# Block 0's tokens kept in pair order through the attention output, with split stores

## The chip, the cores and the metric

The kernel runs on one NeuronCore of a Trainium2 chip. The metric is the device time of one execution in microseconds; what is compared is the median over several runs. The engines are TensorE (PE in the profile, its weight loads PEld), VectorE (DVE), ScalarE (ACT), GpSimd (POOL) and SyncE (SP); each works through its own queue in order, and they wait for one another by semaphores.

## The reference, cut to what matters

Attention with a decay per head runs in blocks over 768 tokens (batch 4, 8 heads of 64), and its output goes through a gated feed-forward layer.

```python
Dmask = np.where(rel >= 0, lam[:, None, None] ** rel[None, :, :], 0.0)      # rel = i - j
for b in range(nb):
    intra = np.einsum('bhic,bhjc->bhij', qb, kb) * Dmask[None]
    intra = np.einsum('bhij,bhjd->bhid', intra, vb)
    inter = np.einsum('bhid,bhde->bhie', qb * lam_pow[None], kv_state)
    out[:, :, sl] = intra + inter
    kv_state = lam_block[None, :, None, None] * kv_state + np.einsum('bhsd,bhse->bhde', kb_dec, vb)
x = np.ascontiguousarray(attn_out.transpose(0, 2, 1, 3)).reshape(B * S, H * D)
gate = 1.0 / (1.0 + np.exp(-(x @ w_gate)))
val = x @ w_val
return gate * val @ w_out                                                     # 3072 x 512
```

The weights are 512 x 1536 (gate and value) and 1536 x 512 (out). The decay is a power of the token distance, so the kernel may use blocks of another size than the reference's 64.

## The kernel before, in words

The tokens are cut into six blocks of 128 (`NSTEP`), each for all four batch rows, so one block is 512 tokens wide in the feed-forward part (`TCH`). The order of all work is written out by hand: the calls at the end of the kernel are emitted in this order, and every engine works through its own part of it.

For blocks 1 to 5 there are pieces: `piece_t` (transposes or scaled queries), `piece_s` (scores), `piece_m` (scores times the decay mask), `piece_a` (value products into `XT`), `c` (state), `piece_gv` (gate and value products, sigmoid, product: one of 12 feature tiles `ft`), and `piece_po` (out projection of one batch row `tt`, an ACT copy into `ob`, and one store on SP's queue).

Block 0 is on its own, since everything waits for it at the start. Its rows are loaded by `load0` with two neighbouring tokens in one partition: partition s of batch row b holds tokens 2s and 2s+1 (`R = 2`, index r), and two batch rows share the 128 partitions (half i of pair bp). `turn0` transposes 64x64 pieces on TensorE (L267), so the columns of a transposed tile are in "pair order": all r = 0 tokens, then all r = 1 tokens. `scale0` (L277, DVE) scales queries by `lam0`, which is in pair order, and `piece_tk0` copies keys (L282, ACT). `piece_s0` makes the scores of one pair of batch rows: 32 products of 64x64 by 64x128 (L295) into four PSUM banks `S0[bp, e, u]`. Its right side is the scaled query tile read with a stride, so that the score columns come out in natural token order. `piece_m0` multiplies by `mask0` (L309 on DVE, or L306 on ACT and L307 on POOL) into `M0[bp]`; `mask0` is made by `make_mask0` from `tri0` (L157). `piece_a0` makes the value products of a pair, again 32 products (L323), in groups of `w` of the four 128-feature groups `m = 2x + u`, and copies them to `XT[0]` (L327 ACT, L328 ACT or DVE).

`idle(n)` emits n products of a zero tile into a scratch bank `wm` (L234, 128x128 by 128x512), which nothing reads. `preload_act_table_set` (L563) loads ACT's table for the sigmoid. PSUM tiles come from two pools, `ps_at` (5 banks, `AT`) and `ps_ff` (3 banks, `FF`). The start, from the second score block to the first gate product:

```python
    piece_s0(1)
    piece_m0(1, 0, 0, True)
    piece_m0(1, 0, 1)
    piece_m0(1, 1, 0)
    piece_m0(1, 1, 1)
    load_w(WV, wv_r, 1, GW)
    piece_a0(0, NMT, [AT, FF])
    idle(3)
    piece_a0(1, 2, [AT] * 4)
    nc.scalar.preload_act_table_set("sigmoid_and_others")
    make_mask(1)
    idle(2)
```

After it come loads on POOL's queue and `gv(0, 0, ..., 6)`, the first gate and value products (L463, L469). Block 0's four output tiles are stored much later, after block 1's gate products.

Of the kernel before, what the change touches and what calls it, by code (L numbers as in the profile page):

```python
# [8 lines left out]
FP32 = mybir.dt.float32  # L9
BF16 = mybir.dt.bfloat16  # L10
AF = mybir.ActivationFunctionType
ALU = mybir.AluOpType
# [4 lines left out]
def kernel(  # L17
# [11 lines left out]
    nc = tc.nc  # L29

    B, H, S, D = q.shape
    C = 128
# [5 lines left out]
    NMT = DM // 128  # L38
# [17 lines left out]
        engines={ET.PE, ET.Pool, ET.DVE, ET.Activation, ET.SP}))  # L56
# [31 lines left out]
    def load_w(t, src, i, w):  # L88
        fs = slice(i * w, (i + 1) * w)
        nc.gpsimd.dma_start(out=t[:, :, fs], in_=src[:, :, fs])  # L90
# [9 lines left out]
    R = 2  # L100
    SR = C // R
    Q0, K0, V0 = (qkv.tile([128, NB2, H, R, D], BF16, tag=c + "b", name=c + "b") for c in "qkv")
# [20 lines left out]
    ip1 = const.tile([128, C], FP32, tag="ip1")  # L123
    nc.vector.memset(ip1[:, 0:1], 1.0)  # L124
    w = 1
# [14 lines left out]
    for r in range(R):  # L140
        nc.vector.tensor_scalar(out=tok[:, 2 + r:3 + r], in0=tok[:, 1:2], scalar1=float(R),
                                scalar2=float(r + 1 - R), op0=ALU.mult, op1=ALU.add)
        nc.vector.tensor_scalar(out=tok[:, 4 + r:5 + r], in0=tok[:, 2 + r:3 + r], scalar1=-1.0,
                                scalar2=None, op0=ALU.mult)
    p1, tj, ntj = tok[:, 0:1], tok[:, 2:4], tok[:, 4:6]
# [5 lines left out]
    for i, src in enumerate((p1, tj[:, 0:1], tj[:, 1:2])):  # L151
        nc.vector.tensor_scalar(out=rem[:, i:i + 1], in0=src, scalar1=-1.0, scalar2=float(C),
                                op0=ALU.mult, op1=ALU.add)
    tri0 = const.tile([128, R, C], FP32, tag="tri0")
    ipr = ip1.rearrange("p (s r) -> p r s", r=R)
    for r in range(R):
        nc.vector.tensor_scalar(out=tri0[:, r], in0=ip1, scalar1=tj[:, r:r + 1], scalar2=None,  # L157
                                op0=ALU.is_ge)

    lnr = const.tile([128, 2, 2, 2], FP32, tag="lnr")  # L160
    for e in range(2):
# [7 lines left out]
    for u in range(2):  # L169
        us = slice(u * 64, (u + 1) * 64)  # L170
# [21 lines left out]
    def make_mask0(e, u):  # L192
        a = 4 * e + 2 * u
        nc.vector.tensor_tensor(
            out=mask0[:, e, u], in0=tri0.unsqueeze(1).to_broadcast([128, 2, R, C]),
            in1=pk0[:, a:a + 2].unsqueeze(3).to_broadcast([128, 2, R, C]), op=ALU.mult)
# [5 lines left out]
    def make_lamq(gs):  # L202
        for g in gs:
            nc.scalar.activation(lamq[:, g], ip1, AF.Exp, scale=lnp[:, g:g + 1])
# [4 lines left out]
    def make_mask(u):  # L209
        nc.vector.tensor_tensor(  # L210
            out=mask[:, u].rearrange("p (e x) c -> p e x c", e=2),
            in0=tri.unsqueeze(1).unsqueeze(1).to_broadcast([128, 2, 2, C]),
            in1=pk.rearrange("p (e u x) -> p u e x", e=2, u=2)[:, u].unsqueeze(3).to_broadcast([128, 2, 2, C]),
            op=ALU.mult)

    def half(e):
        return slice(e * 64, (e + 1) * 64)
# [12 lines left out]
    def idle(n, fresh=False):  # L230
        if fresh:
            wm[0] = ps_ff.tile([128, TCH], FP32, name="wm", tag="ff")
        for i in range(n):
            nc.tensor.matmul(wm[0], lhsT=zero[:, :128], rhs=zero, start=True, stop=True,  # L234
                             skip_group_check=True)

    QS, KS, MT, XT, KD = {}, {}, {}, {}, {}
# [33 lines left out]
    def piece_tq0(b, pool=ps_at, tag="ps"):  # L271
        tp = turn0(Q0, b, pool, tag)
        QS[0, b] = QS0[:, b]
        TQ[b] = tp
# [4 lines left out]
    def piece_tk0(b, pool=ps_at, tag="ps"):  # L279
        tp = turn0(K0, b, pool, tag)  # L280
        KS[0, b] = KS0[:, b]
        nc.scalar.copy(KS[0, b], tp)  # L282

    S0, M0, TQ = {}, {}, {}

    def piece_s0(bp):
        for e in range(2):
            for u in range(2):
                S0[bp, e, u] = ps_at.tile([128, 2, R, C], FP32, name="sp", tag="ps")
        for e in range(2):  # L290
            for x in range(2):
                for r in range(R):
                    for i in range(2):
                        for u in range(2):
                            nc.tensor.matmul(S0[bp, e, u][half(i), x, r, :],  # L295
                                             lhsT=KS[0, 2 * bp + i][half(u), 2 * e + x, r * SR:(r + 1) * SR],
                                             rhs=QS[0, 2 * bp + i][half(u), 2 * e + x, :].rearrange("p (r s) -> p s r", r=R),
                                             start=(x == 0 and r == 0), stop=(x == 1 and r == R - 1),
                                             skip_group_check=True)
        M0[bp] = trsb.tile([128, 2, 2, 2, R, C], BF16, tag="QR", name="MT0", bufs=2)  # L300

    def piece_m0(bp, e, u, pool=False):
        sp = S0[bp, e, u]
        if pool:
            sc = const.tile([128, 2, R, C], FP32, tag="sc", bufs=2)
            nc.scalar.copy(sc, sp)  # L306
            nc.gpsimd.tensor_tensor(out=M0[bp][:, e, u], in0=sc, in1=mask0[:, e, u], op=ALU.mult)  # L307
        else:
            nc.vector.tensor_tensor(out=M0[bp][:, e, u], in0=sp, in1=mask0[:, e, u], op=ALU.mult)  # L309

    def piece_a0(bp, w, banks):
        if 0 not in XT:
            XT[0] = xtp.tile([128, NMT, B, C], BF16, tag="XT", name="XT")
        for m0 in range(0, NMT, w):
            op = []
            for i in range(2):
                pool, tag = banks.pop(0)
                op.append(pool.tile([128, w, C], FP32, name="op", tag=tag))
            for m in range(m0, m0 + w):
                for r in range(R):  # L320
                    for e in range(2):
                        for i in range(2):
                            nc.tensor.matmul(op[i][half(e), m - m0, :], lhsT=V0[half(i), bp, 2 * m + e, r, :],  # L323
                                             rhs=M0[bp][half(i), e, m % 2, m // 2, r, :],
                                             start=(m == m0 and r == 0), stop=(m == m0 + w - 1 and r == R - 1),
                                             skip_group_check=True)
            nc.scalar.copy(XT[0][:, m0:m0 + w, 2 * bp, :], op[0])  # L327
            (nc.vector.tensor_copy if bp else nc.scalar.copy)(XT[0][:, m0:m0 + w, 2 * bp + 1, :], op[1])  # L328

    def piece_t(n, bp):  # L330
        if n > 1:
# [173 lines left out]
    def piece_po(n, tt):  # L505
        po = ps_ff.tile([128, DM], FP32, name="po", tag="ff")
        for ft in range(NFT):
            nc.tensor.matmul(po, lhsT=HT[n, ft][:, tt * 128:(tt + 1) * 128],  # L508
                             rhs=WO[:, ft, :], start=(ft == 0), stop=(ft == NFT - 1))
        ob = osb.tile([128, DM], FP32, tag="ob", name="ob")  # L510
        nc.scalar.copy(ob, po)  # L511
        dst = out[tt * S + n * C:tt * S + (n + 1) * C, :]
        nc.sync.dma_start(out=dst, in_=ob)


    GW = DFF // 6
# [2 lines left out]
    FF = (ps_ff, "ff")  # L519
    AT = (ps_at, "ps")  # L520
# [9 lines left out]
    make_mask0(1, 0)  # L530
    make_tri()
    make_mask(0)
    idle(4)
    piece_tq0(1)
    scale0(1)
    make_mask0(1, 1)
    idle(2)
    piece_tk0(1)
    make_lamq((2, 3))
    idle(1)  # L540
    piece_tq0(2, *FF)
    scale0(2)
    piece_tq0(3, *FF)
    scale0(3)
    piece_s0(0)
    piece_m0(0, 0, 0)
    piece_m0(0, 0, 1)
# [4 lines left out]
    piece_tk0(3, *FF)  # L552
    idle(2, True)
    piece_s0(1)
    piece_m0(1, 0, 0, True)
    piece_m0(1, 0, 1)
    piece_m0(1, 1, 0)
    piece_m0(1, 1, 1)
    load_w(WV, wv_r, 1, GW)
    piece_a0(0, NMT, [AT, FF])  # L560
    idle(3)
    piece_a0(1, 2, [AT] * 4)
    nc.scalar.preload_act_table_set("sigmoid_and_others")  # L563
    make_mask(1)
    idle(2)

# [61 lines left out]
    gvh(1, 1, 0, 1, 2, 3, 4, 5, 6)  # L628
    gv(1, 7, 8, 9, 10, 11)
    piece_po(0, 0)  # L630
    piece_po(0, 1)
    piece_po(0, 2)
    t(2, 0)
    t(2, 1)
# [72 lines left out]
```

## Time and profile before

| what | value |
|---|---|
| median of 6 runs | 231.24 us (230.3 to 231.82) |
| profiled execution, its own time | 231.99 us |
| its span, first to last instruction | 230.2 us, mean granted TensorE clock 0.992 |
| TensorE busy | 220.6 us, 96% of the span |
| DVE, ACT, POOL busy | 102.5, 82.6, 81.0 us |
| score products of block 0 (L295) | 64, 2.7 us busy |
| value products of block 0 (L323) | 64, 2.3 us busy |
| idle products (L234) | 20 recorded, 7.8 us busy, mean 507 ns |
| stores of whole output tiles (L513) | 23 of 256 KB, 2.0 us to landing (median) |

"Busy" is the time in which an engine had an instruction in work; products overlap, so the sum of their own durations is larger. The granted clock is the share of full TensorE clock that was granted in a stretch. The chain of waits goes back from the last instruction, at each step to what released it. "Issue" in it is time in which the engine waited for nothing that the profile shows. A few matmul records may be missing.

### The profile page before, as it was taken

What the parts mean: (1) busy time and instruction counts of PE and PEld (TensorE: products, weight loads), DVE (VectorE), ACT (ScalarE), POOL (GpSimd) and SP (SyncE); (2) the same over time, 40 slices, a digit from 0 to 9 for tenths busy, and PEclk for the clock granted to TensorE, in tenths of its full rate; (3) what the DMA queues carried; (4) which work ended last, traced back from release to release, by engine and by line L of the source; (5) the groups of instructions that cost most, each with busy time, mean ns of one, the idle gap of its engine ahead of it and who ended that gap; (6) DMA issues with size and microseconds to landing.
All of it is one profiled execution on the core that took longest, in us unless ns stands there. A gap on an engine that the chain in (4) does not pass through costs nothing.

```text
span 230.2 us, 4618 instructions
## 1 busy us (share of the span) xinstructions
PE 220.6 (96%) x1921; PEld 113.6 (49%) x1947; DVE 102.5 (45%) x189; ACT 82.6 (36%) x157; POOL 81.0 (35%) x77
## 2 busy tenths in 40 slices
PE   7869999999999999999999999999999999999993
PEld 2635454688544446444446444445444445444442
DVE  7857366484441342334842334842334840334200
ACT  5655324544332224333224433224433225333220
POOL 8979997854950003970003970000000000000000
PEclk9979999999999999999999999999999999999999
DMA  7999999999999912799912899912730012100022
GB/s 67 155 186 156 171 193 159 199 178 157 132 158 154 235 65 77 162 154 147 40 61 80 169 136 146 54 57 82 166 63 3 0 53 86 46 0 0 3 91 93
DMA packets 96517, 24.95 MB, mean 108 GB/s; under 512 B 85616, under 2 KB 93552, under 8 KB 96496
## 3 DMA queue, kind: packets, MB, share of 16 engines
q0 software_dynamic: 76112, 14.16, 89.3%
q1 hardware_dynamic: 20384, 10.49, 19.8%
q8 instruction: 15, 0.25, 0.5%
q14 instruction: 6, 0.05, 0.1%
HBM read 28.32 MB, written 6.29 MB: 150 GB/s over the span
## 4 chain that ended last, share of the span: by engine, by line
PE 92%; DMA 2%; POOL 2%; issue 2%; ACT 1%; DVE 0%; POOLq 0%
PE po L508 26%; PE gp L463 25%; PE vp L469 24%; PE gp L480 3%; PE vp L486 2%; PE sp L356 2%; PE op L384 2%; DMA qb<-in_q_dram 2%; PE op L374 1%; PE po L497 1%; POOL qb L105 1%; PE sp L295 1%; PE cp L450 1%; PE op L323 1%; PE wm L234 1%
## 5 line engine op out<-in xcount | busy, mean ns | idle before, releaser
L472 DVE TENSOR_TENSOR ht<-sg,vp 128x512 bf16<-128x512 bf16 x65 | 44.7, 687 | 76.0 <-PE vp L469 71.8
L463 PE MATMUL gp<-XT,WG 128*128 128x512 bf16 x252 | 66.2, 379 | 0.7 <-issue 0.2
L469 PE MATMUL vp<-XT,WV 128*128 128x512 bf16 x255 | 65.8, 379 | 0.1
L466 ACT ACTIVATE sg<-gp 128x512 bf16<-128x512 f32 x65 | 38.8, 597 | 69.6 <-PE gp L463 69.5
L508 PE MATMUL po<-WO,ht 128*128 128x512 bf16 x266 | 61.3, 379 | 0.5
L508 PEld LDWEIGHTS <-ht 128*128 128x128 bf16 x276 | 26.3, 98 | 31.2
L469 PEld LDWEIGHTS <-WV 128*128 128x128 bf16 x260 | 25.5, 98 | 30.7
L463 PEld LDWEIGHTS <-WG 128*128 128x128 bf16 x260 | 24.9, 98 | 29.4 <-issue 0.2
L511 ACT COPY ob<-po 128x512 f32<-128x512 f32 x23 | 13.5, 585 | 52.5 <-PE po L508 45.8
L364 DVE TENSOR_TENSOR MT<-sp,mask 128x512 bf16<-128x512 f32 x40 | 25.2, 683 | 12.4 <-PE sp L356 12.4
L435 POOL TENSOR_TENSOR sd<-Sb,dec 128x512 f32<-128x512 bf16 x8 | 8.2, 1059 | 48.2 <-DVE Sb L454 48.2
L426 POOL TENSOR_TENSOR kd<-kb,kds 128x1024 bf16<-128x1024 bf16 x6 | 11.3, 1904 | 3.1 <-DMA kb<-in_k_dram 3.1
L454 DVE TENSOR_TENSOR Sb<-cp,sd 128x512 bf16<-128x512 f32 x8 | 5.2, 686 | 15.4 <-PE cp L450 15.4
L393 ACT CAST XT<-op 128x512 bf16<-128x512 f32 x20 | 10.4, 598 | 3.0 <-PE op L384 3.0
L234 PE MATMUL wm<-zero 128*128 128x512 bf16 x20 | 7.8, 507 | 1.7 <-DVE ip L124 1.2
L78 POOL DMA_DIRECT2D qb<-in_q_dram x8 | 9.4, 1182 | 0.0
L84 POOL DMA_DIRECT2D vb<-in_v_dram x6 | 9.3, 1543 | 0.0
L78 POOL DMA_DIRECT2D kb<-in_k_dram x8 | 9.2, 1166 | 0.0
L480 PE MATMUL gp<-XT,WG 128*128 128x256 bf16 x56 | 8.4, 273 | 0.0
L486 PE MATMUL vp<-XT,WV 128*128 128x256 bf16 x56 | 8.4, 273 | 0.0
L490 DVE TENSOR_TENSOR ht<-sg,vp 128x256 bf16<-128x256 bf16 x14 | 5.8, 419 | 5.1 <-PE vp L486 4.0
L483 ACT ACTIVATE sg<-gp 128x256 bf16<-128x256 f32 x14 | 5.4, 384 | 7.0 <-PE gp L480 7.0
(88 smaller groups left out, 146.6 us busy)
## 6 DMA issues: line engine op xcount, KB each, us to landing
out_dram<-ob SPq DMA_DIRECT2D x23, 256.0 KB, 2.0
qb<-in_q_dram POOLq DMA_DIRECT2D x10, 256.0 KB, 9.1
kb<-in_k_dram POOLq DMA_DIRECT2D x10, 256.0 KB, 10.3
vb<-in_v_dram POOLq DMA_DIRECT2D x4, 512.0 KB, 13.3
WG<-in_moe_w_gate_dram POOLq DMA_DIRECT2D x6, 256.0 KB, 7.0
WV<-in_moe_w_val_dram POOLq DMA_DIRECT2D x6, 256.0 KB, 7.2
WO<-in_moe_w_out_dram POOLq DMA_DIRECT2D x3, 512.0 KB, 14.0
qb<-in_q_dram POOLq DMA_DIRECT2D x4, 128.0 KB, 4.5
```

Source lines behind the costliest of these rows:

```text
L78: nc.gpsimd.dma_start(out=lst[n][:, e].rearrange("p b y d -> p (b y) d"), in_=src[:, e::2, sl, :].rearrange("b y s d -> s (b y) d"))
L364: nc.vector.tensor_tensor(out=MT[n, b][:, u], in0=SP[n, b][u], in1=mask[:, u], op=ALU.mult)
L393: nc.scalar.copy(XT[n][:, u::2, 2 * bp:2 * bp + 2, :], OP[bp, u])
L426: nc.gpsimd.tensor_tensor(out=KD[n][:, e], in0=K[n][:, e], in1=kds[:, e::2].unsqueeze(1).unsqueeze(3).to_broadcast([128, B, HP, D]), op=AL ...
L463: nc.tensor.matmul(gp, lhsT=WG[:, mt, fs], rhs=x[:, mt, :], start=(mt == 0), stop=(mt == NMT - 1))
L466: nc.scalar.activation(sg, gp, AF.Sigmoid)
L469: nc.tensor.matmul(vp, lhsT=WV[:, mt, fs], rhs=x[:, mt, :], start=(mt == 0), stop=(mt == NMT - 1))
L472: nc.vector.tensor_mul(HT[n, ft], sg, vp)
L480: nc.tensor.matmul(gp[:, cs], lhsT=WG[:, mt, fs], rhs=x[:, mt, cs], start=(mt == 0), stop=(mt == NMT - 1))
L486: nc.tensor.matmul(vp[:, cs], lhsT=WV[:, mt, fs], rhs=x[:, mt, cs], start=(mt == 0), stop=(mt == NMT - 1))
L508: nc.tensor.matmul(po, lhsT=HT[n, ft][:, tt * 128:(tt + 1) * 128], rhs=WO[:, ft, :], start=(ft == 0), stop=(ft == NFT - 1))
L511: nc.scalar.copy(ob, po)
```

## The change

Block 0's score columns now stay in pair order: `tri0` is made in pair order from the strided view `ipr`, and `piece_s0` reads the scaled queries as they lie. The value products, `XT[0]`, the gate and value products and the output tiles of block 0 then have their tokens in pair order too, and `piece_po` stores each of block 0's tiles with two stores, one for the even and one for the odd tokens (64 partitions each, rows of 2 KB, every other row of the output).

`piece_a0` now goes by `u` (the half of heads) instead of by groups of `m`: pair 0 takes both halves in one go, pair 1 takes `u = 1` first and `u = 0` second, and the engines of the copies are given by the caller. The mask products of pair 1 on DVE change order. The table load moves from behind pair 1's copies to ahead of pair 1's value products. The counts of the idle products change.

```diff
     for r in range(R):
-        nc.vector.tensor_scalar(out=tri0[:, r], in0=ip1, scalar1=tj[:, r:r + 1], scalar2=None,
-                                op0=ALU.is_ge)
+        nc.vector.tensor_scalar(out=tri0[:, r].rearrange("p (r s) -> p r s", r=R), in0=ipr,
+                                scalar1=tj[:, r:r + 1], scalar2=None, op0=ALU.is_ge)
...
-                                             rhs=QS[0, 2 * bp + i][half(u), 2 * e + x, :].rearrange("p (r s) -> p s r", r=R),
+                                             rhs=QS[0, 2 * bp + i][half(u), 2 * e + x, :],
...
-    def piece_a0(bp, w, banks):
+    def piece_a0(bp, us, banks, engines):
         if 0 not in XT:
             XT[0] = xtp.tile([128, NMT, B, C], BF16, tag="XT", name="XT")
-        for m0 in range(0, NMT, w):
-            op = []
-            for i in range(2):
-                pool, tag = banks.pop(0)
-                op.append(pool.tile([128, w, C], FP32, name="op", tag=tag))
-            for m in range(m0, m0 + w):
+        op = []
+        for i in range(2):
+            pool, tag = banks.pop(0)
+            op.append(pool.tile([128, len(us), 2, C], FP32, name="op", tag=tag))
+        for j, u in enumerate(us):
+            for x in range(2):
                 for r in range(R):
                     for e in range(2):
                         for i in range(2):
-                            nc.tensor.matmul(op[i][half(e), m - m0, :], lhsT=V0[half(i), bp, 2 * m + e, r, :],
-                                             rhs=M0[bp][half(i), e, m % 2, m // 2, r, :],
...
+                            nc.tensor.matmul(op[i][half(e), j, x, :],
+                                             lhsT=V0[half(i), bp, 2 * (2 * x + u) + e, r, :],
+                                             rhs=M0[bp][half(i), e, u, x, r, :],
...
-            nc.scalar.copy(XT[0][:, m0:m0 + w, 2 * bp, :], op[0])
-            (nc.vector.tensor_copy if bp else nc.scalar.copy)(XT[0][:, m0:m0 + w, 2 * bp + 1, :], op[1])
+        for i in range(2):
+            dst = XT[0].rearrange("p (x u) b c -> p u x b c", u=2)[:, us[0]:us[-1] + 1, :, 2 * bp + i, :]
+            engines[i](dst if len(us) > 1 else dst[:, 0], op[i] if len(us) > 1 else op[i][:, 0])
...
-        nc.sync.dma_start(out=dst, in_=ob)
+        if n > 0:
+            nc.sync.dma_start(out=dst, in_=ob)
+            return
+        for r in range(R):
+            nc.sync.dma_start(out=dst.rearrange("(s r) m -> r s m", r=R)[r],
+                              in_=ob[r * SR:(r + 1) * SR, :])
...
     make_mask(0)
-    idle(4)
+    idle(2)
     piece_tq0(1)
     scale0(1)
     make_mask0(1, 1)
-    idle(2)
+    idle(1)
     piece_tk0(1)
     make_lamq((2, 3))
-    idle(1)
     piece_tq0(2, *FF)
...
     piece_m0(1, 0, 1)
+    piece_m0(1, 1, 1)
     piece_m0(1, 1, 0)
-    piece_m0(1, 1, 1)
     load_w(WV, wv_r, 1, GW)
-    piece_a0(0, NMT, [AT, FF])
-    idle(3)
-    piece_a0(1, 2, [AT] * 4)
+    idle(1)
+    sc_, ve_ = nc.scalar.copy, nc.vector.tensor_copy
+    piece_a0(0, (0, 1), [AT, FF], [sc_, sc_])
     nc.scalar.preload_act_table_set("sigmoid_and_others")
+    idle(1)
+    piece_a0(1, (1,), [AT, AT], [sc_, sc_])
+    piece_a0(1, (0,), [AT, AT], [sc_, ve_])
     make_mask(1)
     idle(2)
```

More of the change, by code (lines that the diff above doesn't have):

```diff
@@ L322, in piece_a0 @@
                         for i in range(2):
-                            nc.tensor.matmul(op[i][half(e), m - m0, :], lhsT=V0[half(i), bp, 2 * m + e, r, :],
-                                             rhs=M0[bp][half(i), e, m % 2, m // 2, r, :],
-                                             start=(m == m0 and r == 0), stop=(m == m0 + w - 1 and r == R - 1),
+                            nc.tensor.matmul(op[i][half(e), j, x, :],
+                                             lhsT=V0[half(i), bp, 2 * (2 * x + u) + e, r, :],
+                                             rhs=M0[bp][half(i), e, u, x, r, :],
+                                             start=(j == 0 and x == 0 and r == 0),
+                                             stop=(j == len(us) - 1 and x == 1 and r == R - 1),
                                              skip_group_check=True)
-            nc.scalar.copy(XT[0][:, m0:m0 + w, 2 * bp, :], op[0])
-            (nc.vector.tensor_copy if bp else nc.scalar.copy)(XT[0][:, m0:m0 + w, 2 * bp + 1, :], op[1])
+        for i in range(2):
+            dst = XT[0].rearrange("p (x u) b c -> p u x b c", u=2)[:, us[0]:us[-1] + 1, :, 2 * bp + i, :]
+            engines[i](dst if len(us) > 1 else dst[:, 0], op[i] if len(us) > 1 else op[i][:, 0])
     def piece_t(n, bp):
```

## The prediction

> **What bounds the kernel now.** I read the page first, then the chain of waits, then the busy times by window, then ACT's and PE's timelines. TensorE is busy 96% of the span, so what can move the time is a stretch where its queue stands still or its clock is low. The clock row shows one such place after the start:
>
> ```profile
> PEclk9979999999999999999999999999999999999999
> ```
>
> The fourth slice (17.3 to 23.0 us) has recovered, the third (11.5 to 17.3) has not. The chain of waits over that place, start and length in us:
>
> ```profile
> 4.76 4.98 DMA qb<-in_q_dram
> ...
> 11.41 0.58 ACT KS L282
> 12.00 0.49 ACT sc L306
> 12.49 0.50 ACT KS L282
> ...
> 13.03 1.10 PE sp L295 x29
> 14.13 0.23 PE op L323 x12
> 14.36 0.80 issue
> 15.16 0.75 PE op L323 x19
> 15.90 0.33 issue
> 16.24 1.06 PE wm L234 x2
> 17.30 1.00 PE op L323 x24
> ```
>
> Up to 9.7 us the chain is the landing of the last query row. Then come block 0's first scores (L295), three ACT copies, the second scores, value products (L323), idle products (`wm`), value products, and at 18.67 us the first gate product, from where TensorE is dense to the end. So the change is worth what it does to that 18.67, plus what it does to the clock. The busy times by window (start:end, length, PE, PEld, DVE, ACT, POOL, granted clock, DMA share, GB/s) are cut where the clock was seen to change, 3.41 us apart:
>
> ```profile
> 4.61:8.03 3.42, 2.62 (x54) 1.50 (x55) 3.20 (x8) 2.86 (x12) 3.42 (x6) 1.00 1.42 136
> 8.03:11.44 3.41, 3.10 (x110) 2.42 (x111) 2.82 (x7) 1.94 (x8) 3.41 (x6) 1.00 1.69 165
> 11.44:14.85 3.41, 2.21 (x62) 1.49 (x58) 2.27 (x4) 2.12 (x4) 2.08 (x3) 1.00 1.62 182
> 14.85:18.27 3.42, 2.78 (x54) 1.66 (x55) 1.13 (x3) 1.43 (x3) 3.42 (x5) 0.50 1.33 175
> 18.27:21.68 3.41, 3.37 (x19) 1.53 (x17) 3.09 (x4) 2.49 (x5) 3.41 (x5) 1.00 1.28 155
> ```
>
> Read down PE busy and clock: windows with 2.62 and 3.10 busy were followed by full clock, the one with 2.21 by a window at 0.50, the one with 2.78 at half clock by full clock again. I take this as: under some point between 2.21 and 2.62 busy of 3.41, the next window runs at half rate. Last, ACT and PE around the value products:
>
> ```profile
> 15.94 0.58 ACT L327 CAST XT<-op 128x512 bf16<-128x512 f32 x1 [1.61 <-PE op L323]
> 16.42 0.59 ACT L328 CAST XT<-op 128x512 bf16<-128x512 f32 x1
> 17.91 0.80 ACT L327 CAST XT<-op 128x256 bf16<-128x256 f32 x2 [0.90 <-PE op L323]
> 18.73 1.28 ACT L563 ACT_TABLE_LOAD   x1
> 13.03 1.17 PE L295 MATMUL sp<-QS,KS 64*64 64x128 bf16 x30 [0.57 <-ACT KS L282]
> 17.23 1.07 PE L323 MATMUL op<-MT,vb 64*64 64x128 bf16 x32
> ```
>
> The table load stands behind the copies, where only the first sigmoid waits for it. And 30 score products at full clock take longer than 32 value products of the same shape at half clock; their difference is the strided right-hand side of the scores.
>
> **The change, part by part.** All sums are against this execution (span 230.2, own time 231.99); the median of the six runs is 231.24, 0.75 lower, and I put the difference on that median.
>
> *Scores with a contiguous right side.* A block of 32 at half clock takes 1.07, of which 0.31 is the last product's own time, so 0.76 of issue; at full clock I halve that and add 0.28: 0.66 (estimate) against 1.17. First block: done at about 10.7 instead of 11.2. Behind it stand the transposes of the third key row (10.94), which also need their load (issued 5.42; key loads land 4.7 after, median; 6.9 at most on that line): gain 0 to 0.4, I take 0.4, the median being nearer. The three ACT copies follow in their 1.56, so the second score block starts at 12.6 instead of 13.03.
>
> *Idle products: ten become five* (4, 2, 1 ahead of the scores become 2, 1, 0; one comes ahead of pair 0's value products; three after them become one). Each takes 0.22 at full and 0.43 at half clock (3.57 for eight at the start). Those before 9.7 us stand beside the query landing: their removal gives no time. What they did is fill windows. In the second window I now count 2.62 less three of 0.22, plus 0.35 for the second key transposes that move in: 2.3, in the unknown strip. In the third: transposes 0.44, then 9.78 to 10.7, transposes 0.44 and 0.19: 2.0, under 2.21.
>
> *Value products.* Same 64, by halves; the mask products swapped in order (three of 0.69 either way). Block pair 1 needs the fourth value row, issued at 8.76, landing by the 6.9 at most: 15.7. So TensorE can't start pair 1 before about 15.6, though the row before shows it at 17.23.
>
> *ACT's order.* This is what I weigh most. The table load (1.28) now stands between pair 0's copies and pair 1's, and pair 1 has three copies on ACT instead of two. The first gate product reads feature group 0, which is in the half computed and copied last; before, groups 0 and 1 were copied first. So from the end of pair 0's value products to the first gate product lie 1.07 (two copies) + 1.28 + 0.80 + 0.43 = 3.6 us in one engine's line, with TensorE waiting.
>
> *The unexplained 0.80 "issue"* in the middle of pair 0's products has no releaser in the trace. It may stay (0.8) or go (0); I take 0, since fewer instructions stand ahead of it, and keep 0.8 for the range.
>
> *Rest.* The triangle with a strided read (0.33 each, at most doubled) feeds a scaled query at 6.29 that is wanted at 9.94: nothing; without that 3 us cover it would be 0.7. Four more stores are 0.33 each on SP, while block 0's tiles come 2.6 apart from 70.92; the transposes behind them on that queue go out at 93.16. The load of the second WV slice stands behind POOL's mask product and moves up with it. The Trainium skill (DMA: Bandwidth & Descriptors, Rules for kernel authors) advises against two transfers to disjoint partition halves, because they serialize, which speaks against the split stores; by it they would be dearer, but the trace has 2.0 to 6.0 us of landing under dense TensorE work, and the sum stays without them.
>
> *Sum of the likeliest case.* Third window 2.0, so 11.44 to 14.85 runs at half clock. Scores 12.6 to 13.4 (issue), idle 0.43, pair 0 0.76 and its last product: end at 14.95. Plus 3.6: first gate product at 18.55, which I round to no gain (18.6). The half-clock window is dense, so full clock returns at 14.85; then TensorE has pair 1 (0.66) and two idle products (0.6): 1.3 of 3.41 busy, far under 2.21. The next window, 18.27 to 21.68, runs at half clock, now under dense gate products: from 18.6 that is 3.1 us at half rate, 1.5 lost. Sum +1.5: 231.24 + 1.5 = 232.7 (span 231.7, own time 233.5). If the second window already falls under the point, 8.03 to 11.44 is slow, mostly beside the loads; the first gate product comes at 18.3 and the later dip costs 1.7: +1.3. With the 0.8 kept, the start is 19.4 and the dip costs 1.15: +1.9.
>
> The Trainium skill (TensorE: Matmul & The Clock Gate, Why this matters for your kernels) asks only that idle gaps of TensorE stay under some 3 us. By that rule neither kernel would lose its clock here and the sum would be near 0. The row stands against it: the clock fell at 14.85 after a window whose longest gap inside was 0.57.
>
> **The rivals.** *One, on the other side: the dip falls where TensorE waits anyway, or nowhere.* If 2.0 busy is still enough, the scores and pair 0 run at full clock: scores 12.6, pair 0 ends 14.05, first gate product 17.65, 1.0 earlier. Then either nothing falls (-1.0), or 14.85 to 18.27 does, with pair 1 1.07, idle 1.06 and 0.6 of gate products, 2.7 busy, so it recovers and costs 0.3 (-0.7). It decides if the point of the drop lies under 2.0; against it stands the 2.21 row. Time 230.2 to 230.5. *Two: no further dip, but ACT's line sets the start.* Then 18.6 to 19.4: 0 to +0.8, so 231.2 to 232.0. For it: the rule of windows rests on four rows. *Three: the scores do not get faster*, because weight loads set their pace (0.87 for 30 in the PEld row beside them). Then pair 0 ends 0.4 later and the window counts 2.4: +0.4 without a dip, +1.7 with one.
>
> **How the numbers follow.** Forecast 0.55 (+1.3 to +1.9), rival one 0.25, two 0.14, three 0.06. About 0.3% (0.69 us) is what a measurement of this kernel can tell from no change. Faster: rival one but for its edge, 0.23. Same: that edge and half of two, 0.09. Slower: the rest, 0.68. Range: from 230.3 (nearly all of rival one) to 233.2 (+1.9 and a little of the 0.6 by which runs lie above their median); the forecast's own range is 232.4 to 233.2.
>
> **What would show it.** Right: a score block of 32 under 0.8 us at clock 1.00; clock 0.50 in a window that ends by 14.85 and again in 18.27 to 21.68, gate products 0.43 apart there; ACT's table load ahead of three short copies, and the first gate product waiting for an ACT copy at 18.3 to 19.4. Wrong: a first gate product under 18 with full clock after it; clock low in one window only, before 18.3; or a new wait past 30 us, on weights or stores, which I hold to be hidden.

## The result and the profile after

The changed kernel takes 231.72 us (median of 29 runs, 230.67 to 234.03), the kernel before, run beside it, 230.67 us (64 runs): a ratio of 1.005 [1.0033, 1.0067], or 1.05 us slower between the medians. Medians are over all runs of a kernel; ratios come with a 95% interval, leave out the few runs over 1.5% above the fastest of their kernel, and are not quotients of these medians. The profiled execution of after has an own time of 234.03 us and a span of 232.3; it is the longest of the 29, and that of before lay 1.3 above its median, so the two traces show the mechanisms better than the typical size. They differ by 2.04 us in span (230.22 and 232.26), in three parts:

| stretch, us | before | after | difference |
|---|---|---|---|
| start to first gate product | 18.67 | 19.89 | +1.22 |
| first gate product to TensorE's last product | 207.64 | 209.32 | +1.68 |
| TensorE's last product to the end of the span (the tail) | 3.91 | 3.06 | -0.85 |

The page of after, TensorE's busy time and the granted clock in 40 slices of 5.8 us:

```profile
PE 222.4 (96%) x1916; PEld 114.4 (49%) x1942; DVE 100.8 (43%) x188; ACT 82.8 (36%) x158; POOL 81.1 (35%) x77
...
PEclk9997999999999999999999999999999999999999
```

The dent has moved from the third slice to the fourth, where the gate products run. The chain of waits of after (start, length, engine, what) over the same place as before:

```profile
4.77 5.64 DMA qb<-in_q_dram
...
12.27 0.59 ACT KS L282
...
13.89 1.06 PE sp L295 x30
14.95 0.54 PE wm L234
15.49 1.05 PE op L323 x32
16.54 1.06 ACT XT L331 x2
17.61 0.02 issue
17.62 1.28 ACT L570
18.91 0.01 issue
18.92 0.93 ACT XT L331 x3
19.85 0.04 issue
19.89 1.54 PE gp L466 x4
21.43 1.71 PE vp L472 x4
23.14 1.19 PE gp L466 x4
```

Before, the chain went through TensorE here. Now ACT carries it for 3.35 us, from the end of pair 0's products to the first gate product: two copies, the table load (L570), three copies. The stop of 0.80 called "issue" is gone. A group of four gate or value products (`gp`, `vp`), elsewhere 0.86, takes 1.54 and 1.71. The busy times by window (start:end, length, PE, PEld, DVE, ACT, POOL, clock, DMA share, GB/s) say why:

```profile
13.43:16.84 3.41, 2.90 (x65) 1.97 (x66) 1.90 (x4) 1.30 (x3) 2.88 (x3) 1.00 1.47 192
16.84:20.26 3.42, 1.55 (x36) 0.88 (x37) 1.02 (x2) 2.97 (x6) 3.42 (x6) 1.00 1.06 130
20.26:23.67 3.41, 3.41 (x10) 1.18 (x8) 0.42 (x1) 0.60 (x1) 3.41 (x3) 0.50 1.24 159
```

While ACT works through its line, TensorE is busy 1.55 of 3.42 us; the next window, full of gate products, has half the clock. This half-clock window under gate products is called the dip below. (The 1.00 in the first row is a default: the records of the clock begin at 16.84. The paces show half clock up to there: idle products take 0.61 to 0.63 us each, and 0.38 to 0.39 behind it; the chain has 30 contiguous products of the second score block in 1.06, where 29 take 0.45 at full clock, below. So a mean clock of a run counts a start without records as full.)

### The profile page after: what moved, and what is told of

Same layout as the page of the kernel before. It is cut to its first block, busy times and chain, and to the rows that moved or that the text cites. A ratio compares the mean times of both kernels' runs of the same rounds, so it can differ in the third digit from the quotient of the medians.

```text
span 232.3 us, 4620 instructions
## 1 busy us (share of the span) xinstructions
PE 222.4 (96%) x1916; PEld 114.4 (49%) x1942; DVE 100.8 (43%) x188; ACT 82.8 (36%) x158; POOL 81.1 (35%) x77
## 4 chain that ended last, share of the span: by engine, by line
PE 91%; ACT 3%; DMA 2%; POOL 2%; issue 1%; DVE 0%; POOLq 0%
PE po L511 26%; PE gp L466 25%; PE vp L472 24%; PE gp L483 3%; PE vp L489 2%; DMA qb<-in_q_dram 2%; PE sp L359 2%; PE op L387 2%; PE op L377 1%; PE po L500 1%; POOL qb L105 1%; PE cp L453 1%; ACT XT L331 1%; PE sp L295 1%; POOL kb L105 1%
## 5 line engine op out<-in xcount | busy, mean ns | idle before, releaser
L466 PE MATMUL gp<-XT,WG 128*128 128x512 bf16 x252 | 67.1, 383 | 2.6 <-ACT XT L331 1.8
L472 PE MATMUL vp<-XT,WV 128*128 128x512 bf16 x255 | 66.5, 383 | 0.0
L234 PE MATMUL wm<-zero 128*128 128x512 bf16 x15 | 7.1, 591 | 1.2 <-DVE ip L124 1.2
```

What stands on the lines that cost most here:

```text
L466: nc.tensor.matmul(gp, lhsT=WG[:, mt, fs], rhs=x[:, mt, :], start=(mt == 0), stop=(mt == NMT - 1))
L472: nc.tensor.matmul(vp, lhsT=WV[:, mt, fs], rhs=x[:, mt, :], start=(mt == 0), stop=(mt == NMT - 1))
```

## The experiments

Each kernel was timed beside the kernel before; unless said otherwise the profile is of one run.

**The table load alone.** From after, back behind pair 1's copies:

```diff
     piece_a0(0, (0, 1), [AT, FF], [sc_, sc_])
-    nc.scalar.preload_act_table_set("sigmoid_and_others")
...
     piece_a0(1, (0,), [AT, AT], [sc_, ve_])
+    nc.scalar.preload_act_table_set("sigmoid_and_others")
```

> The changed kernel with ACT's table load put back behind pair 1's copies. Theory ACT line (the table load and three copies in a row after pair 0 set the first gate product, and the wait starves TensorE so that a half-clock window falls under dense gate products): the first gate product waits 1.3 us less after pair 0's copies, the time falls by 1.0 to 1.3 us against the changed kernel and comes to -0.3 to +0.2 us of the kernel before. Theory idle counts (fewer idle products at the start leave the clock low during scores and value products, and that is what costs): within 0.3 us of the changed kernel, so about +1 us against before. Theory split stores: also +1 us against before.

230.29 us, ratio 0.9978 [0.9953, 1.0004]; the interval lies clear of after's. 0.9978 against 1.005 is 0.72% or 1.66 us, and 1.43 lie between the medians: moving this one line is worth more than the whole loss of 1.05. In its chain the table load is gone from between the copies:

```profile
15.67 0.70 PE op L323 x32
16.36 0.02 issue
16.39 0.42 DVE XT L331
16.81 0.61 DVE mask L210
17.42 1.02 PE gp L466 x4
```

**The token order alone** (before, with `tri0`, the scores' right side and the split stores of the change):

```diff
-    rhs=QS[0, 2 * bp + i][half(u), 2 * e + x, :].rearrange("p (r s) -> p s r", r=R),
+    rhs=QS[0, 2 * bp + i][half(u), 2 * e + x, :],
...
-        nc.sync.dma_start(out=dst, in_=ob)
+        if n > 0:
+            nc.sync.dma_start(out=dst, in_=ob)
+            return
+        for r in range(R):
+            nc.sync.dma_start(out=dst.rearrange("(s r) m -> r s m", r=R)[r],
+                              in_=ob[r * SR:(r + 1) * SR, :])
```

> The kernel before with pair order alone: triangle in pair order, contiguous right side of the scores, two stores per tile of block 0; value products, copies, table load and idle products as before. Theory ACT line: a score block of 32 takes about 0.66 us at full clock instead of 1.17, the second block starts 0.4 us earlier, the first gate product 0.4 to 0.9 us earlier, time -0.3 to -0.9 us against before. Theory idle counts: 0 to -0.9. Theory split stores: +0.5 to +1 us.

229.59 us, 0.9961 [0.9933, 0.999]: faster by 0.4%. But not through the scores: in its profile the first gate product stands at 18.40, 0.27 earlier than in the profile of before but 1.31 later than with the stores split and nothing else (17.09, below), with a stop of 1.21 us ahead of it; the tail is 3.08.

**The idle counts alone** (before, with after's counts):

```diff
-    idle(4)
+    idle(2)
...
-    idle(2)
+    idle(1)
...
-    idle(1)
...
+    idle(1)
     piece_a0(0, NMT, [AT, FF])
-    idle(3)
+    idle(1)
```

> The kernel before with the changed kernel's idle counts alone (2, 1, 0 ahead of the scores, 1 ahead of pair 0's value products, 1 after them). Theory ACT line: pair 1 starts up to 0.8 us earlier since two idle products fewer stand ahead of it, a half-clock window may come earlier beside the loads; time -0.6 to +0.3 us against before. Theory idle counts: +0.7 to +1.3 us, with more of the start at half clock. Theory split stores: 0.

230.72 us, 1.0004 [0.9982, 1.0027]: no difference that shows. Its profile has half clock from 8.33 to 15.16 us, and yet the first gate product at 17.13, within 0.04 of a trace that was at full clock from 3.94 on (17.09, the split stores alone, below): its chain goes through the query load (4.77 to 9.71) and, behind the scores, through an ACT copy and POOL's mask product (14.06 to 15.99).

**The value products by halves alone** (before, with `piece_a0`, the mask order and the table load of the change; the idle counts of before):

```diff
-    piece_a0(0, NMT, [AT, FF])
-    idle(3)
-    piece_a0(1, 2, [AT] * 4)
+    piece_a0(0, (0, 1), [AT, FF], [sc_, sc_])
     nc.scalar.preload_act_table_set("sigmoid_and_others")
+    idle(3)
+    piece_a0(1, (1,), [AT, AT], [sc_, sc_])
+    piece_a0(1, (0,), [AT, AT], [sc_, ve_])
```

> The kernel before with the value products, copies and mask order by halves and the table load ahead of pair 1's value products; token order, stores and the numbers of idle products (4, 2, 1, and 3 after pair 0) as before. Theory ACT line: the first gate product comes about 3.6 us after pair 0's end, near 19.5 us, so +0.9 us, and +0.5 to +1.5 more where a half-clock window then falls under gate products: +0.9 to +2.0 us against before. Theory idle counts: 0 to +0.3. Theory split stores: 0.

232.14 us, 1.0055 [1.0029, 1.008]: the whole loss, in a kernel whose clock is 1.00 from 4.07 us on in its profile. The chain:

```profile
14.47 0.40 issue
14.87 0.52 PE op L323 x19
15.39 1.06 ACT XT L331 x2
...
16.46 1.28 ACT L565
...
17.76 0.93 ACT XT L331 x3
18.69 0.04 issue
18.73 1.02 PE gp L466 x4
```

Again 3.34 us from pair 0's end (15.39) to the first gate product. The line on ACT costs this without any dip. The order of the mask products changes here with the halves and was not tried by itself.

**Which part of the order helps: stores or scores.** After with whole stores, and before with nothing but the stores split (halves of natural rows, 64 partitions each). The first edit is against after, the second against before:

```diff
-        for r in range(R):
-            nc.sync.dma_start(out=dst.rearrange("(s r) m -> r s m", r=R)[r],
-                              in_=ob[r * SR:(r + 1) * SR, :])
+        nc.sync.dma_start(out=dst, in_=ob)
```

```diff
-        nc.sync.dma_start(out=dst, in_=ob)
+        if n > 0:
+            nc.sync.dma_start(out=dst, in_=ob)
+            return
+        for r in range(R):
+            nc.sync.dma_start(out=dst[r * SR:(r + 1) * SR, :], in_=ob[r * SR:(r + 1) * SR, :])
```

> The changed kernel with one store per tile of block 0; the rows of block 0 are left in pair order in the output, so the putting back of the rows is left out. In the traces so far TensorE takes 207.63 us from the first gate product to its end in the kernels without a late half-clock window, with either kind of store, and from TensorE's end to the end of the span pass 3.9 us with whole stores (before, idle counts, halves) and 3.1 us with split stores (changed kernel, table late, order only). Theory end of queue (the four extra stores change what SP has to wait through after the last store): the tail goes back to 3.9 us and the time rises by 0.8 us against the changed kernel, to about +1.9 us of before. Theory split stores cost: the time falls by 0.5 to 1 us against the changed kernel. Theory that the tail has another cause (pair order, chance): within 0.3 us of the changed kernel.

> The kernel before with block 0's stores split into two halves of rows, everything in natural order, nothing else changed. Theory end of queue: tail 3.1 us instead of 3.9, time -0.8 us against before, with the start of the gate products unchanged. Theory split stores cost: +0.5 to +1 us. Theory other cause: 0.

After with whole stores: 232.35 us, 1.0089 [1.0057, 1.0121], tail 3.88. Before with split stores: 230.2 us, 0.9971 [0.9941, 1.0001], tail 3.07. So four stores more, issued some 150 us earlier, shorten the tail by 0.8 us. The waits of SP's queue over the last 10 us (engine, line, what is waited for: us in total, times, longest), first before, then the split stores alone:

```profile
SPq L702 <- DMA out_dram<-ob: 1.3, 2, 1.0
```

```profile
SPq L706 <- DMA out_dram<-ob: 0.5, 2, 0.3
```

At the end SP walks through nine waits for semaphores (SP's queue has 85 instructions in all with whole stores and 91 with split ones). In all six traces with whole stores the last store's semaphore stands third in this list, in all eight with split ones seventh. With whole stores SP spends the longest wait, 1.0, on the store before the last, and still has six waits to walk through when the last has landed, one of them of 0.48: its queue ends 0.97 after the last landing (229.35 against 228.38) in before and 0.21 after it (231.45 against 231.24) in after. The shorter tail is shown by eight kernels with split stores, at 3.06 to 3.09, and six with whole ones, at 3.88 to 3.91; that the place of the last store in this list makes it is argued from the order of the waits, and no run moved that place alone.

The profile of the split stores alone also shows the start of before without a dip:

```profile
13.16 1.10 PE sp L295 x29
...
14.49 0.38 issue
14.87 0.47 PE op L323 x19
15.34 0.75 PE wm L234 x3
16.10 0.57 PE op L323 x32
16.67 0.54 PE wm L234 x2
17.20 0.91 PE gp L463 x4
```

Nothing of the start was edited in this kernel, and its first gate product stands at 17.09 (18.67 in the profile of before). The stretch from there to TensorE's end is 207.63 here and 207.64 in before.

**The order with whole stores**, which leaves the scores' gain by itself (before, with two of the edits of the order alone):

```diff
-        nc.vector.tensor_scalar(out=tri0[:, r], in0=ip1, scalar1=tj[:, r:r + 1], scalar2=None,
-                                op0=ALU.is_ge)
+        nc.vector.tensor_scalar(out=tri0[:, r].rearrange("p (r s) -> p r s", r=R), in0=ipr,
+                                scalar1=tj[:, r:r + 1], scalar2=None, op0=ALU.is_ge)
...
-    rhs=QS[0, 2 * bp + i][half(u), 2 * e + x, :].rearrange("p (r s) -> p s r", r=R),
+    rhs=QS[0, 2 * bp + i][half(u), 2 * e + x, :],
```

> Order only, but with one store per tile of block 0; the rows of block 0 stay in pair order in the output, so the putting back of the rows is left out. It tells the contiguous scores apart from the stores. Theory scores pay: 29 score products go from 0.91 to 0.45 us in each block, the first gate product comes 0.3 to 0.5 us earlier, time -0.3 to -0.5 us against before, tail 3.9 us. Theory swallowed (the loads of keys and values and POOL's mask product hold what the scores give): -0.2 to +0.2 us.

230.98 us, 1.0005 [0.9973, 1.0038]: no gain from the faster scores shows, though the interval reaches down to -0.6 us; nor does the order with split stores (0.9961) stand apart from the split stores alone (0.9971). The chain shows the scores faster, and what eats it:

```profile
10.39 0.45 PE sp L295 x29
...
12.31 1.28 POOL MT L307
...
13.63 0.25 PE op L323 x3
13.88 1.54 issue
15.42 0.74 PE op L323 x19
```

29 products take 0.45 us instead of 0.91. Pair 0 begins earlier, and stops for 1.54 instead of 0.80. The stop has the same place in every trace that has it: TensorE's 225th weight load, in the middle of pair 0 (13 products in, or 16 where fewer instructions stand ahead). It ends 2.3 to 2.5 us after a packet of 16 KB on the queue that the page calls "instruction" begins: 12.75 and 15.16 in before, 13.12 and 15.42 here, 13.87 and 16.18 with the order and split stores, 12.42 and 14.88 with split stores alone. In the four traces without the stop, after among them, TensorE gets there later than that. Ten traces thus agree with a wait of TensorE for its own instructions; that the packet holds them is argued, and no experiment moved it by itself.

**Filling the hole with products.** After, with six idle products instead of two at the end, so that TensorE is busy while ACT works:

```diff
     make_mask(1)
-    idle(2)
+    idle(6)
```

> The changed kernel with six instead of two idle products after pair 1's value products, in the stretch where TensorE waits for ACT's last copy (four more are 0.9 us at full and 1.7 us at half clock, the wait is 1.8 us). Theory ACT line with a dip: the first gate product starts as before the edit, but runs with a half-clock window under gate products get fewer; median 0.3 to 0.8 us below the changed kernel, its slowest runs (above 233 us) gone. If the dip doesn't hang on the hole: 0 to +0.3 us.

231.73 us, 1.0038 [1.0011, 1.0066]. The median didn't fall: a miss. The chain has idle products where after waited, and full gate products behind them:

```profile
18.12 2.47 PE wm L234 x6
20.59 0.86 PE gp L466 x4
21.46 0.86 PE vp L472 x4
```

In this profile the clock is at half up to 20.26, so six idle products take 2.47 and now hold the first gate product themselves, until 20.43 (19.89 in after): the hole is filled, and the start is no shorter. All 12 spans lie between 229.1 and 231.1, where 6 of after's 29 lie at 231.3 and above. If nothing had changed, 12 in a row below would happen about once in 16 times ((23/29)^12 = 0.06): a hint that the longest runs of after are those with the dip, and no more.

**More products early**, to lift the clock before the score blocks (after, with 4, 2 and 1 idle products as before):

```diff
-    idle(2)
+    idle(4)
...
-    idle(1)
+    idle(2)
...
+    idle(1)
```

> The changed kernel with the early idle products of before (4, 2, 1 instead of 2, 1, 0), nothing else changed. Theory that the idle counts matter together with ACT's line (pair 0's end moves with the clock, and the line of 3.6 us hangs on it): less half clock in the runs' means (changed kernel mostly 6.9 us, kernel before mostly under 2), -0.3 to -0.7 us against the changed kernel. Theory that they don't matter: within 0.2 us of the changed kernel.

233.36 us (6 runs, 232.93 to 233.95), 1.0116 [1.0081, 1.0151]: neither theory expected a loss. The start of the profiled run is faster, as hoped: pair 0 ends at 15.51, the first gate product stands at 18.86. The dip then meets the gate products, in windows that begin elsewhere:

```profile
12.25:15.66 3.41, 2.93 (x66) 1.98 (x66) 1.89 (x3) 1.30 (x4) 2.73 (x3) 0.50 1.55 184
15.66:19.08 3.42, 1.40 (x36) 0.79 (x36) 1.02 (x2) 3.12 (x6) 3.42 (x5) 1.00 1.36 178
19.08:22.49 3.41, 3.41 (x10) 1.21 (x9) 0.12 (x1) 0.60 (x1) 3.41 (x4) 0.50 1.27 159
```

The stretch from the first gate product to TensorE's end is 209.32 again, 1.69 above 207.63. Without the dip such a run would span 229.55 us (18.86 + 207.63 + 3.06), or 230.58 with after's later start; all six spans lie between 231.1 and 232.2, so by this working each had it. Why the early idle products make it so frequent stays open.

**The table late and the read order** (the kernel with the late table, whose first gate tile reads groups 1, 3, 0, 2, so that the half copied first is read first):

```diff
-        for mt in range(NMT):
+        mts = (1, 3, 0, 2) if n == 0 and ft == 0 else (0, 1, 2, 3)
+        for mt in mts:
...
-                             start=(mt == 0), stop=(mt == NMT - 1))
+                             start=(mt == mts[0]), stop=(mt == mts[-1]))
```

> The changed kernel with the table load behind pair 1's copies and the first gate tile reading feature groups 1, 3, 0, 2, so that it begins with the half that is copied first. Theory ACT line: the first gate product waits for pair 1's first two copies only, 0.3 us earlier than with the table late alone; time -0.2 to -0.4 us against that kernel, -0.7 to -0.9 us against before. Theory idle counts: no difference from the table late alone.

230.22 us, 0.997 [0.9941, 0.9999], against 0.9978 without it: no difference that shows, neither for nor against the 0.2 to 0.4 us expected.

**The halves with the table late** (the halves alone, table load moved as in the first experiment):

```diff
-    nc.scalar.preload_act_table_set("sigmoid_and_others")
     idle(3)
     piece_a0(1, (1,), [AT, AT], [sc_, sc_])
     piece_a0(1, (0,), [AT, AT], [sc_, ve_])
+    nc.scalar.preload_act_table_set("sigmoid_and_others")
```

> Halves only, with the table load behind pair 1's copies. Theory ACT line: the table load's 1.28 us leave the line, -1.2 to -1.6 us against halves only, so -0.2 to +0.3 us against before. Theory that the halves themselves cost (the first gate product reads the half copied last, three copies on ACT): +0.5 us or more against before remains.

230.98 us, 1.0031 [1.0, 1.0062], against 1.0055 [1.0029, 1.008]. In the profiles the first gate product moves by what was expected, from 18.73 to 17.47:

```profile
16.51 0.92 ACT XT L331 x3
...
17.47 1.02 PE gp L466 x4
```

The ratio moves by 0.24%, half of that, the medians by 1.16 us, and the intervals overlap: the direction fits, the size is open. So is what the halves cost without the table load: the interval leaves anything from nothing to 0.6%.

**A version that beats both.** The order with split stores, `piece_a0` and the table load of before, and one idle product instead of three between the pairs:

```diff
-    idle(3)
+    idle(1)
```

> Order only with one idle product instead of three between the pairs' value products, as a better version of both. Theory that these idle products stand on TensorE's path when the clock is full (0.75 us for three in the run with split stores alone): 0.3 to 0.5 us below order only, -1.2 to -1.4 us against before. If the fourth value row's landing near 15.5 us holds pair 1 anyway: as order only, -0.9 us.

229.52 us, 0.9938 [0.9901, 0.9976], the lowest of all; the interval overlaps that of the order alone (0.9961), so what the idle products add isn't shown. Its profiled run, above the median at 231.78, has the longest of the stops:

```profile
14.19 2.03 issue
16.23 0.74 PE op L323 x19
```

## Why the prediction was right, and where its steps were not

231.72 us lies in the range, and the change is slower, as forecast; the size was +1.05 where +1.5 was forecast. The size owes something to luck. The forecast's own range, 232.4 to 233.2, was missed; 231.72 lies in the range of the second rival, no further dip with ACT's line setting the start (231.2 to 232.0). And all sums stood on 231.24, a median of six runs, where 64 runs gave 230.67. The steps:

- **ACT's line: right, and the main cost.** Forecast 3.6 us from pair 0's end to the first gate product, 3.35 in after and 3.34 with the halves alone. The three copies took 0.93, not 1.23. The halves and the table load alone gave the whole loss, and taking the table load out of the changed kernel's line gave back more than it.
- **"No gain at the start": the step that failed on size.** I compared 18.6 with the 18.67 of one execution that had itself a half-clock window, 14.85 to 18.27, where TensorE was needed. Without that window the same work starts its gate products at 17.09 (of the 1.58 between them, 0.29 lies ahead, in the stop that ended at 15.16 and not at 14.87). So ACT's line costs the typical run more at the start than I said. The medians tell the same: own time less 1.77 (231.99 - 230.22), the tail and 207.63 gives a start of 17.36 for before (230.67 - 1.77 - 3.91 - 207.63) and 19.26 for after (231.72 - 1.77 - 3.06 - 207.63), if the median run has no dip later: +1.90 at the start and -0.85 at the end, +1.05. These are estimates: the same working gives 17.73 for the split stores alone, whose start is that of before. In the profile of after the sum was short in one term more: pair 0 ended at 16.54 and not at 14.95, with the query row landed at 10.41 (9.74 in before) and the whole start at half clock.
- **The dip under the gate products: it exists, its frequency was wrong.** In the profile it came while ACT's line kept TensorE waiting, 1.68 against 1.5 forecast, though later than in the sum (20.26 to 23.67, not 18.27 to 21.68), and by their spans in all six runs with the early idle products. I took its windows of 3.41 us from one trace as if they hung on the first product. They don't: in the five kernels that start as after does, up to pair 0's products, the first record of full clock begins at 16.84, 4.95, 5.66, 20.26 and 4.92 us (after, table late, whole stores, filled hole, read order). Where a window falls decides whether the dip meets the gate products, and by the spans it did so fully in about 6 of 29 runs. As a term that always applies, 1.5 was too much; with the baseline that was too late, the two errors nearly cancelled.
- **The point of the drop: not confirmed.** I gave a strip from 2.21 to 2.62 busy of 3.41 us, under which the next window would run at half clock. Windows with 2.21, 1.55 and 1.40 were followed by half clock. But so was one with 2.51 (the first row, with the early idle products), while windows with 1.84 and 2.41 were followed by full clock (the second row, with the order alone, and the third, with the halves alone):

```profile
8.84:12.25 3.41, 2.51 (x98) 1.82 (x98) 3.11 (x6) 1.98 (x6) 2.97 (x5) 1.00 1.74 174
13.77:17.18 3.41, 1.84 (x64) 1.26 (x65) 2.05 (x4) 1.13 (x4) 3.11 (x4) 1.00 1.44 195
17.73:21.14 3.41, 2.41 (x12) 1.10 (x12) 0.45 (x2) 1.54 (x5) 3.41 (x5) 1.00 1.25 153
```

So no busy time parts the two, and a dip can't be foretold from it; nor does it say when the clock comes back, since after stayed at half clock over windows with 2.56 and 2.62 busy. What decides stays open. The rule of the Trainium skill that I weighed (TensorE: Matmul & The Clock Gate, Why this matters for your kernels), gaps under some 3 us, is contradicted by the runs: the longest gap ahead of the dip was 1.78 in after and 1.86 with the early idle products.

- **The scores: right in duration, wrong in place.** Half the time, as forecast; but the 0.4 us that I put on the path are swallowed by the stop in the middle of pair 0, at a ratio of 1.0005. That stop is the 0.80 "issue", which I took as gone because fewer instructions stand ahead. It is gone in after, because TensorE arrives too late to meet it.
- **The stores: wrong sign.** I costed them at nothing behind 2.0 to 6.0 us of landing, and gave no bound below nothing. They take 0.8 us off the tail. I had asked whether their transfers were hidden, and not what more stores do to the end of SP's queue. The Trainium skill (DMA: Bandwidth & Descriptors, Rules for kernel authors) says that transfers to disjoint partition halves serialize; that they would be dearer was my reading of it. As transfers they gained nothing here either: in the split stores alone, the eight halves landed 5.7 us after their issue (median), block 0's whole tiles in before 3.2 to 6.0. The gain lies in the waits at the end, and the kernel with nothing else changed is at 0.9971 [0.9941, 1.0001].
- **The idle products: right that fewer cost no time by themselves** (1.0004). With ACT's line behind them they count: the changed kernel with the early ones put back is at 1.0116, against 1.005.

The parts and the whole differ by no more than the noise. Order -0.39%, idle counts +0.04%, halves with table load +0.55% make +0.20%, and +0.50% was measured; the three intervals (0.28, 0.23 and 0.26% to a side) leave the sum open by some 0.4%, an estimate. If there is a rest, two things can hold it: ACT's line hangs on pair 0's end, which comes later where the start runs at half clock (16.54 in after, 15.39 with the halves alone), and the later dip; how much each gives stays open.

## What to carry to other kernels

Before a term is put on one trace, ask in which state of the clock that trace was: here the baseline of the sum, 18.67, lay 1.6 us above a second profile of the same start (17.09). An operation that is moved ahead is paid when the only engine that can release the bottleneck has to pass it: 1.28 us of table load here. A store whose transfer is long hidden can still change the end, in the queue that waits for all stores there (0.8 us here).

## What the hardware showed that I had not expected

TensorE stopped for 0.1 to 2.0 us in ten of 14 traces, always at the same place of its stream and until 2.3 to 2.5 us after a packet on the queue called "instruction" began; score products ahead of it that took half the time gave no gain that shows. That it waits for its own instructions is the likely reading.

The granted clock changes in steps of 3.41 us in every trace, and among kernels with the same start it first stands at full anywhere from 4.92 to 20.26 us. Half clock beside the loads was free (from 8.33 to 15.16 us in the idle counts alone, at a ratio of 1.0004); one window of it under dense products costs 1.7 us, and the one from 14.85 to 18.27 in the profile of before came with a start 1.6 us later.
